# Batch 0's first tile alone and batch 1's expert tile by tile: another order for the first 48 slots of an attention and MLP kernel

## Chip, core and metric

The kernel runs on one core of a Trainium2 chip. The metric is the device time of one execution in microseconds (us). The engines are PE (TensorE, matmuls), DVE (VectorE), ACT (ScalarE), POOL (GpSimd, which here mostly issues loads) and SP (SyncE, which issues stores and DMA transposes). Each works through its own list of instructions in order and waits on semaphores for the others.

## What is computed

The inputs are q, k, v (8 batches, 8 heads, 576 rows, 64 columns), two vectors of gains and two weights, 512x2048 and 2048x512.

```python
kv = np.einsum('bhsd,bhse->bhde', k, v)
out = np.einsum('bhsd,bhde->bhse', q, kv)
rms = np.sqrt(np.mean(out * out, axis=-1, keepdims=True) + 1e-06)
x = out / rms * g_norm                     # heads side by side: (8, 576, 512)
...
xn = (x - mu) / np.sqrt(var + 1e-06) * g_ln
ch = np.maximum(xn @ w_ch1, 0.0) @ w_ch2
return x + ch
```

## The kernel before

**Tiles.** A batch's 576 rows make four tiles of 128 rows and a rest of 64; the rests of two batches share a tile of their own ("rem"). Per tile, `Tile` makes: `o` (four matmuls of q transposed with kv of a pair of heads), `sq` (square, ACT), `red` (sum per head, DVE), `root` (ACT), `inv` (reciprocal, DVE), `y` and `x` (scale by inverse root and by g_norm, DVE, with the sum for the mean), `xc` (minus mean, times g_ln, bf16, DVE), `var` (ACT), and `turn` (four transposes on PE into PSUM and an ACT copy to xT, or a DMA transpose). `o_g` with `x_g` is a shorter way for batch 0: kv is multiplied by g_norm beforehand (`kv_g`), so that one matmul and one DVE instruction give x.

**Expert.** `mm1` (line 402) multiplies xT by the first weight, in groups that fill one PSUM bank of 128x512 (16 matmuls of 128 columns for one tile, 8 of 256 columns for two tiles together), and ACT evicts each with Relu (line 405). `mm2_part` (line 418) multiplies by the second weight, 16 matmuls of 512 columns per tile, and `finish` (DVE, line 423) adds x and stores.

**Order.** It is written out by hand. `tick()` is called ahead of each group of the first product and each four matmuls of the second. Each call is a slot with a number; `at(slot, fn)` puts other work ahead of the slot's matmuls. A batch of four tiles takes 32 slots: 0 to 15 are the first product of batch 0, 16 to 31 its second product, 32 to 47 the first product of batch 1. `plan_tile(s, ...)` puts o, sq and red at slot s, y, x and xc at s + behind, var at s + 6, and turn at its own slot. `q_turns` transposes batch 1's q on PE, `kv_of` makes kv of a batch; both use the single PSUM bank of `ps_m` ("misc"), as `turn` does. `ps1` has three banks, `ps2` and `ps_out` two each.

**Start.** k comes by SP and ACT, cast on the chip; v and q by POOL in its queue (lines 126 to 132): v in two halves of two pairs of heads, q's lower part (five groups j of 64 rows, on partitions 0 to 63) in two halves of four heads, the first quarter of the first weight, q's upper part (four groups j, on partitions 64 to 127), the rest of the first weight, the second weight, batch 1. PE runs 18 matmuls whose result is not read (`fill`, line 196) until v is there. `kv_first` makes kv in two halves of two pairs. Tiles 0 and 1 of batch 0 then go side by side in halves of four heads: `half_turn` (q transposed), `half_o` (o and square), `half_red`; then root, o_g, x_g, and xc in halves of 256 columns (`halves_xc`, `halves_turn`). Tile i is made of two groups j: tile 0 of j 0 and 1, tile 1 of j 2 and 3 of the lower part; tiles 2 and 3 of the upper part. The fifth lower group is the rest J.

In slots 0 to 15 the first product of batch 0 runs over tiles 0 and 1 in pieces (`mm1(0, ts, 1, c0, c1)`), then tile 2, then tile 3. Slot 1 holds the turn of tile 2's q, tile 1's transposes, and tile 2's o to xc; slots 4 and 5 do the same for tile 3; slots 6 and 10 turn tiles 2 and 3; slot 9 turns J. Batch 1's tiles begin at slots 23, 25, 29 and 33 and are turned at 28, 31, 37 and 39; its first product takes tiles 0 and 1 together (slots 32 to 39), then 2 and 3 (slots 40 to 47).

Of the kernel before, what the change touches and what calls it, by code (L numbers as in the profile page):

```python
# [14 lines left out]
def kernel(  # L15
# [11 lines left out]
    nc = tc.nc  # L27
    f32 = mybir.dt.float32
    bf16 = mybir.dt.bfloat16
# [9 lines left out]
    nDe = Dh // 128  # L39
# [46 lines left out]
    def lo(t, b, h0=0, h1=H):  # L86
        return t[b, h0:h1, :S_LO, :].rearrange("h (p j) d -> p h j d", j=JJ)
# [29 lines left out]
    def pairs(t, hp0, hp1):  # L117
        return bass.AP(tensor=t.tensor, offset=t.offset + hp0 * 2 * S * D,
                       ap=[[JP * D, 128], [2 * S * D, hp1 - hp0], [1, JP * D]])
# [3 lines left out]
    nc.vector.memset(fill_sb, 0.0)  # L123
    nc.sync.dma_start(k_f[:, :HP // 2], pairs(k, 0, HP // 2))
    nc.scalar.dma_start(k_f[:, HP // 2:], pairs(k, HP // 2, HP))
    nc.gpsimd.dma_start(v_p[:, :HP // 2], pairs(v, 0, HP // 2))
    nc.gpsimd.dma_start(v_p[:, HP // 2:], pairs(v, HP // 2, HP))
    for h0 in (0, H // 2):
        nc.gpsimd.dma_start(q_in[0][:64, h0:h0 + H // 2], lo(q, 0, h0, h0 + H // 2))
    load_w1(0)  # L130
    make_identity(nc, identity)
    nc.gpsimd.dma_start(q_in[0][64:, :, :J], up(q, 0))
# [57 lines left out]
        n = turn_groups(tp, i, 0, H)  # L190
        copy(qts[0][:, i, :, :n], tp[:, :, :n])  # L191

    def fill(n, pool=ps2, tag="p2"):
        for _ in range(n):
            p1 = pool.tile([128, 512], f32, tag=tag, name="p1")
            nc.tensor.matmul(p1, lhsT=fill_sb[:, :128], rhs=fill_sb, start=True, stop=True)  # L196
            del p1

    def turn_q_dma(b):
        q_p = kv_in.tile([128, JJ, H, D], bf16, tag="qp", bufs=2)  # L200
# [3 lines left out]
            q_t.rearrange("p j hp t -> p (j hp) t"), q_p.rearrange("p j h d -> p (j h d)"))  # L204
        qts[b] = q_t

    def kv_first():
        kvp = held[0] = kv_pack[0]
        g = g_norm_sb.to_broadcast([128, HP // 2, D])
        for i, (pe, te, po, to) in enumerate(((ps_m, "misc", ps1, "p1"), (ps1, "p1", ps1, "p1"))):  # L210
            even = pe.tile([128, HP // 2, D], f32, tag=te, name="even")
            odd = po.tile([128, HP // 2, D], f32, tag=to, name="odd")
            hps = slice(i * HP // 2, (i + 1) * HP // 2)
            for hp in range(hps.start, hps.stop):
                for j in range(JP):
                    js = slice(j * D, (j + 1) * D)
                    for hh, dst in ((0, even), (1, odd)):
                        rows = slice(hh * D, hh * D + D)
                        nc.tensor.matmul(dst[rows, hp - hps.start, :], lhsT=k_p[rows, hp, js],
                                         rhs=v_p[rows, hp, js],  # L220
                                         start=(j == 0), stop=(j == JP - 1))
            nc.vector.tensor_copy(kvp[:D, hps, :D], even[:D])
            nc.scalar.copy(kvp[D:, hps, D:], odd[D:])
            nc.vector.tensor_mul(kv_g[:D, hps, :D], even[:D], g[:D])
            nc.vector.tensor_mul(kv_g[D:, hps, D:], odd[D:], g[D:])
            del even, odd

    def kv_of(b):
        kv_ps = ps_m.tile([128, HP, D], f32, tag="misc", name="kv_ps")
# [127 lines left out]
            blks["rem"] = new_block("rem", 1)  # L357
        return Tile(mms, blks["rem"], b // 2)

    def plan_tile(s, make, turn_at, on_pe, behind=2):  # L360
        box = []

        def first():
            t = make()
            box.append(t)
            t.o()
            t.sq()
            t.red()

        def second():  # L370
            t = box[0]
            t.y()
            t.x()
            t.xc()

        def third():
            box[0].var()

        def fourth():
            box[0].turn(on_pe)  # L380

        at(s, first)
        at(s + behind, second)
        at(s + 6, third)
        at(turn_at, fourth)

# [71 lines left out]
    def at(slot, fn):  # L458
        agenda.setdefault(int(slot), []).append((slot, fn))
# [12 lines left out]
    del gl_row  # L472

    qts[0] = qt_pool.tile([128, JJ, HP, 128], bf16, tag="qt", name="qt")
    fill(18)
    kv_first()


    t = [main_tile(0, i, ps2, "p2") for i in range(4)]
    for i in range(2):  # L480
        t[i].ss = work.tile([128, H, 1], f32, tag="ss", bufs=4, name="ss")
    sqs = [work.tile([128, H, D], f32, tag="sq", name="sq") for _ in range(2)]
    banks = (((ps_out, "ops"), (ps_m, "misc")), ((ps_out, "ops"), (ps1, "p1")))
    copies = ((nc.scalar.copy, nc.scalar.copy), (nc.vector.tensor_copy, nc.vector.tensor_copy))

    def half_turn(half):
        hp0 = half * HP // 2
        tps = [ps2.tile([128, HP // 2, 128], bf16, tag="p2", name="tp") for _ in range(2)]
        for i in range(2):
            turn_groups(tps[i], i, 2 * hp0, 2 * hp0 + H // 2)  # L490
        for i in range(2):
            copies[half][i](qts[0][:, i, hp0:hp0 + HP // 2], tps[i])

    def half_o(i, half):
        hp0 = half * HP // 2
        pool, tag = banks[half][i]
        o = pool.tile([128, H // 2, D], f32, tag=tag, name="o_half")
        flat = o.rearrange("p h e -> p (h e)")
        for k2 in range(HP // 2):
            nc.tensor.matmul(flat[:, k2 * 128:(k2 + 1) * 128], lhsT=qts[0][:, i, hp0 + k2, :],  # L500
                             rhs=kv_pack[0][:, hp0 + k2, :], start=True, stop=True)
        nc.scalar.activation(sqs[i][:, half * H // 2:(half + 1) * H // 2], o, func=AF.Square)

    def half_red(i, half):
        hs = slice(half * H // 2, (half + 1) * H // 2)
        nc.vector.tensor_reduce(t[i].ss[:, hs], sqs[i][:, hs], axis=AX.X, op=ALU.add)

    half_turn(0)
    fill(2, ps_out, "ops")
    half_o(0, 0)  # L510
    half_turn(1)
    half_o(1, 0)
    half_o(0, 1)
    half_red(0, 0)
    half_red(0, 1)
    half_o(1, 1)
    t[0].root()
    half_red(1, 0)
    half_red(1, 1)
    t[0].o_g(ps1, "p1")  # L520
    t[1].o_g(ps1, "p1")
    fill(8)
    t[0].x_g()
    t[1].root()


    def halves_xc(i):
# [5 lines left out]
                                           in1=g_ln_sb[:, cs], op0=ALU.add, op1=ALU.mult)  # L533
            yield xc

    def halves_turn(i, xcs, pool, tag):
        xT = t[i].blk[2]
        for c, xc in enumerate(xcs):
            tp = pool.tile([128, 2, 128], bf16, tag=tag, name="tp")
            for kk in range(2):  # L540
                nc.tensor.transpose(tp[:, kk, :], xc[:, kk * 128:(kk + 1) * 128], identity)
            nc.scalar.copy(xT[:, 2 * c:2 * c + 2, i * 128:(i + 1) * 128], tp)

    halves_turn(0, halves_xc(0), ps_out, "ops")
    t[1].x_g()
    xc1 = list(halves_xc(1))


    def x2():
        t[2].red()  # L550
        t[2].y()
        t[2].x()
        t[2].xc()

    def x3():
        t[3].sq()
        t[3].red()
        t[3].y()
        t[3].x()
        t[3].xc()  # L560

    def o2():
        t[2].o()
        t[2].sq()

    def next_loads():
        nc.gpsimd.memset(k_in[0][64:, :, J], 0.0)
        nc.gpsimd.memset(v_in[0][64:, :, J], 0.0)
        load_batch(2)

    at(1, lambda: turn_first(2, ps_m, "misc", nc.vector.tensor_copy))
    at(1.1, lambda: halves_turn(1, xc1, ps_out, "ops"))
    at(1.2, o2)
    at(1.3, x2)
    at(4, lambda: turn_first(3, ps_m, "misc"))
    at(5, lambda: t[3].o())
    at(5.1, x3)
    at(6, lambda: t[2].turn(True))
    at(9, lambda: turn_first(J, ps_m, "misc"))
    at(9.5, next_loads)  # L580
    at(10, lambda: t[3].turn(True))
    for i in range(4):
        at(16 + i, lambda i=i: t[i].var())
    at(20, lambda: (rstd_of(0), t.clear()))
# [2 lines left out]
    def q_turns(s, b):  # L587
        def start():
            q_ps[b] = kv_in.tile([128, JJ, H, D], bf16, tag="qp", bufs=2, name="q_p")
            nc.vector.tensor_copy(q_ps[b].rearrange("p j h d -> p h j d"), q_in[b % NB])  # L590
            qts[b] = qt_pool.tile([128, JJ, HP, 128], bf16, tag="qt", name="qt")
            turn_q(b, 0, ps_out, "ops")
            turn_q(b, 1, ps_out, "ops")

        at(s, start)
        for i, j in enumerate((2, 3, 4)):
            at(s + 1.5 + i, lambda j=j: turn_q(b, j, ps_m, "misc"))
        at(s + 4, lambda: q_ps.pop(b))

    at(21, lambda: kv_of(1))  # L600
    q_turns(21.5, 1)
    for j, s, behind, tn in ((0, 23, 1, 28), (1, 25, 1, 31), (2, 29, 2, 37), (3, 33, 2, 39)):
        plan_tile(s, lambda j=j: main_tile(1, j), tn, True, behind)
    at(46, lambda: rstd_of(1))

    at(36, lambda: kv_of(2))
# [19 lines left out]
    at(32 * B + 14, lambda: rstd_of("rem"))  # L626


    for ts, c0, c1 in ((0, 0, 8), (1, 0, 8), (0, 8, 12), (1, 8, 12), (0, 12, 16), (1, 12, 16),
                       (2, 0, 16), (3, 0, 16)):  # L630
        mm1(0, ts, 1, c0, c1)
    p2s = [ps1.tile([128, Dm], f32, tag="p1", name="p2") for _ in range(2)]
    p2s += [ps2.tile([128, Dm], f32, tag="p2", name="p2") for _ in range(2)]
    for ts in range(4):
        mm2_part(0, ts, p2s[ts], 0, nDe // 2)
    for ts in range(4):
        p2 = p2s[ts]
        p2s[ts] = None
        mm2_part(0, ts, p2, nDe // 2, nDe)
        finish(0, ts, p2)  # L640
        del p2
    del blks[0], m1s[0]
    mm1(1, 0, 2)
    mm1(1, 2, 2)
    mm2(1)
    mm1(2, 0, 2)
    mm1(2, 2, 2)
# [36 lines left out]
```

## Time and profile before

| | |
|---|---|
| median of three runs | 293.75 us (293.29, 293.94, 293.75) |
| the profiled execution | 293.29 us, of which the span of the profile is 291.2 us |
| DVE, ACT busy | 151.0 us, 155.8 us |
| PE, first product (line 402) | 889 matmuls recorded, 131.1 us |
| PE, second product (line 418) | 590 matmuls recorded, 126.6 us |
| granted TensorE clock | 1.00 in every stretch |
| first matmul of slot 0, 16, and o in slot 48 | 15.75, 33.34 and 68.20 us |

In a timeline each row is: start, duration, engine, line, operation, written tile <- read tiles, shapes, count; in brackets the idle time of the engine before it and what ended that. The duration of a row on PE includes the modelled tail of its last matmul, so that rows overlap. Some matmul records are missing, so counts can be one short. In the chain each row is: start, duration, and the engine, tile and line that the end depended on in that stretch.

### The profile page before, as it was taken

To read this page: it belongs to the slowest core of one execution; us is meant where nothing else is said; L and a number is where in the kernel's file an instruction comes from. 1 tells how busy PE (TensorE), PEld (TensorE's weight loads), DVE (VectorE), ACT (ScalarE), POOL (GpSimd) and SP (SyncE) were. 2 spreads that over 40 slices of the span, in tenths; PEclk is the share of its full clock that TensorE was granted. 3 is DMA by queue.
4 is the path that set the end of the run, shared out by engine and by line. 5 is a ranking of instruction groups with operands and counts; after the bars stand their busy time and mean duration, and the time that the engine had idled before them with its cause. 6 is when DMAs were issued, how large, how long until landed. Compare 5 with 4: busy or idle time off the path is not lost.

```text
span 291.2 us, 5506 instructions
## 1 busy us (share of the span) xinstructions
PE 280.6 (96%) x2158; PEld 156.8 (54%) x2184; DVE 151.0 (52%) x335; ACT 155.8 (54%) x339; POOL 41.3 (14%) x68
## 2 busy tenths in 40 slices
PE   8889999989999999999999999999999999999995
PEld 3579754876569744444444444444444444444444
DVE  5775029917997793576257935752578300220022
ACT  3467765776459841892189408930894066017500
POOL 8523520004014002300320014000000000000000
PEclk9999999999999999999999999999999999999999
DMA  7999999559999948994998279928202510131033
GB/s 214 203 206 203 201 202 203 114 92 150 168 192 137 166 60 147 200 172 85 138 211 118 56 139 174 201 60 168 66 18 44 120 36 0 38 75 33 0 73 74
DMA packets 64377, 36.08 MB, mean 124 GB/s; under 512 B 31836, under 2 KB 59356, under 8 KB 64352
## 3 DMA queue, kind: packets, MB, share of 16 engines
q0 software_dynamic: 28016, 17.76, 43.4%
q1 hardware_dynamic: 35824, 17.25, 30.5%
q10 hardware_dynamic: 512, 0.72, 0.8%
q8 instruction: 17, 0.28, 0.4%
q14 instruction: 8, 0.07, 0.1%
HBM read 36.71 MB, written 9.44 MB: 158 GB/s over the span
## 4 chain that ended last, share of the span: by engine, by line
PE 87%; DVE 5%; DMA 2%; ACT 2%; issue 1%; POOL 1%; DVEq 0%; POOLq 0%
PE p L402 40%; PE p L418 40%; PE o_ps L260 3%; DMA q_in<-in_q_dram 2%; PE kv_ps L235 2%; DVE o_sb L423 1%; DVE ss L287 1%; DVE xc L321 1%; DVE x_blk L311 1%; DVE y L292 1%; PE tp L183 1%; ACT m L405 1%; PE p L196 1%; PE tp L337 0%; PE tp L170 0%
## 5 line engine op out<-in xcount | busy, mean ns | idle before, releaser
L402 PE MATMUL p<-xT_blk,w_sb 128*128 128x512 bf16 (+2 forms) x889 | 131.1, 302 | 1.4 <-ACT xT_blk L339 0.8
L418 PE MATMUL p<-w_sb,m 128*128 128x512 bf16 (+2 forms) x590 | 126.6, 368 | 1.5 <-issue 0.8
L405 ACT ACTIVATE m<-p 128x512 bf16<-128x512 f32 x144 | 85.5, 596 | 44.2 <-PE p L402 42.1
L402 PEld LDWEIGHTS <-w_sb 128*128 128x128 bf16 x896 | 76.1, 98 | 46.3 <-issue 1.6
L418 PEld LDWEIGHTS <-m 128*128 128x128 bf16 x608 | 57.0, 98 | 61.8
L423 DVE SCALAR_TENSOR_TENSOR o_sb<-p,rstd,x_blk 128x512 f32<-128x512 f32 (+2 forms) x38 | 27.4, 721 | 53.2 <-PE p L418 50.3
L266 ACT ACTIVATE sq<-o_ps 128x512 f32<-128x512 f32 x34 | 20.2, 594 | 40.6 <-PE o_ps L260 40.5
L287 DVE TENSOR_REDUCE ss<-sq 128x8 f32<-128x512 f32 x34 | 23.1, 678 | 14.0 <-ACT sq L266 14.0
L329 ACT ACTIVATE dev<-x_blk,st_blk 128x512 f32<-128x512 f32 x36 | 25.7, 715 | 5.1 <-DVE st_blk L315 4.9
L321 DVE SCALAR_TENSOR_TENSOR xc<-x_blk,st_blk,g_ln_sb 128x512 bf16<-128x512 f32 x34 | 25.6, 752 | 1.2
L292 DVE TENSOR_TENSOR y<-o_ps,inv 128x512 f32<-128x512 f32 x34 | 23.5, 692 | 3.1
L311 DVE SCALAR_TENSOR_TENSOR x_blk<-y,g_norm_sb 128x512 f32<-128x512 f32 x34 | 23.5, 692 | 1.2
L411 DVE RECIPROCAL rstd<-rstd 128x4 f32<-128x4 f32 x9 | 1.6, 174 | 35.2 <-ACT rstd L410 35.2
L304 DVE RECIPROCAL inv<-rms 128x8 f32<-128x8 f32 x36 | 7.2, 201 | 22.9 <-ACT rms L297 22.9
L98 POOL COPY gate<-qt 1x1 bf16<-1x1 bf16 x5 | 0.9, 178 | 115.6 <-DMA qt<-q_p 115.6
L297 ACT ACTIVATE rms<-ss,eps_sb 128x8 f32<-128x8 f32 x36 | 10.7, 297 | 10.3 <-DVE ss L287 9.6
L260 PEld LDWEIGHTS <-qt 128*128 128x128 bf16 (+1 forms) x152 | 9.8, 100 | 7.1 <-issue 1.7
L260 PE MATMUL o_ps<-kv_pack,qt 128*128 128x128 bf16 (+1 forms) x152 | 13.3, 220 | 0.3 <-DVE qt L191 0.2
L196 PE MATMUL p<-fill_sb 128*128 128x512 bf16 x27 | 8.5, 476 | 1.4 <-DVE eps_sb L137 1.2
L329 ACT ACTIVATION_READ_ACCUMULATOR dev<-x_blk,st_blk 128x1 f32 x36 | 6.8, 190 | 0.0
L235 PEld LDWEIGHTS <-k_in 128*64 128x64 bf16 x280 | 5.0, 112 | 2.8 <-issue 2.8
L238 ACT CAST kv_pack<-kv_ps 64x256 bf16<-64x256 f32 x7 | 2.6, 365 | 7.2 <-PE kv_ps L235 7.2
(79 smaller groups left out, 117.4 us busy)
## 6 DMA issues: line engine op xcount, KB each, us to landing
out_dram<-o_sb SPq DMA_DIRECT2D x70, 128.0 KB, 2.4
w_sb<-in_moe_w_ch_dram POOLq DMA_DIRECT2D x8, 512.0 KB, 14.3
k_in<-in_k_dram POOLq DMA_DIRECT2D x7, 320.0 KB, 5.9
v_in<-in_v_dram POOLq DMA_DIRECT2D x7, 320.0 KB, 9.6
q_in<-in_q_dram POOLq DMA_DIRECT2D x7, 320.0 KB, 12.7
q_in<-in_q_dram POOLq DMA_DIRECT2D x8, 256.0 KB, 13.2
k_in<-in_k_dram POOLq DMA_DIRECT2D x7, 256.0 KB, 7.0
v_in<-in_v_dram POOLq DMA_DIRECT2D x7, 256.0 KB, 10.9
```

Source lines behind the costliest of these rows:

```text
L196: nc.tensor.matmul(p1, lhsT=fill_sb[:, :128], rhs=fill_sb, start=True, stop=True)
L260: nc.tensor.matmul(flat[rows, hp * 128:(hp + 1) * 128], lhsT=lhsT_of(hp), rhs=kvp[:, hp, :], start=True, stop=True)
L266: nc.scalar.activation(self.sq_t, self.o_ps, func=AF.Square)
L287: nc.vector.tensor_reduce(self.ss, self.sq_t, axis=AX.X, op=ALU.add)
L292: nc.vector.tensor_mul(self.y_t, self.o_ps, self.inv().to_broadcast([128, H, D]))
L311: nc.vector.scalar_tensor_tensor(x_blk[:, ts].rearrange("p (h d) -> p h d", h=H), in0=self.y_t, scalar=1.0, in1=g_norm_sb.to_broadcast([12 ...
L321: nc.vector.scalar_tensor_tensor(self.xc_t, in0=x_blk[:, self.ts], scalar=st[:, 1, self.ts:self.ts + 1], in1=g_ln_sb, op0=ALU.add, op1=ALU ...
L329: nc.scalar.activation(dev, x_blk[:, ts], func=AF.Square, bias=st[:, 1, ts:ts + 1], accum_out=st[:, 2, ts:ts + 1])
L402: nc.tensor.matmul(p1[:, i, :], lhsT=w1_sb[:, kk, de * 128:(de + 1) * 128], rhs=blk[2][:, kk, sl], start=(kk == 0), stop=(kk == nK - 1))
L405: nc.scalar.activation(m1[:, de0:de0 + per, sl], p1, func=AF.Relu)
L418: nc.tensor.matmul(p2[:, c0:c1], lhsT=m1s[b][:, de, ts * 128:(ts + 1) * 128], rhs=w2_sb[:, de, c0:c1], start=(de == 0), stop=(de == nDe - 1))
L423: nc.vector.scalar_tensor_tensor(o_sb[:, c0:c1], in0=p2[:, c0:c1], scalar=rstds[b][:, ts:ts + 1], in1=blks[b][0][:, ts, c0:c1], op0=ALU.mu ...
```

## The change

1. Loads: v comes as three pairs of heads and one pair; between the two, q's groups j 0 and 1 of all heads; after the last pair, q's groups j 2 to 4.
2. `kv_first` becomes the class `KvFirst`: three pairs (kv_a), then tile 0's turn of q, one fill, and the last pair (kv_b).
3. Tile 0 goes alone, its o, square and reduce in parts of three pairs and one pair. Tile 1's q is turned behind tile 0's o; its o, square and o_g, and the turn of J, stand behind tile 0's o_g with three and five fills around; its reduce comes behind tile 0's xc.
4. Slot 1 turns q of tiles 2 and 3 at once, tile 1's two halves (the second copied by DVE) with tile 2's o between them, and ends with tile 2's root. Tile 2 goes by o_g and x_g (slot 2). Tile 3's o to xc come right behind tile 2's turn (slot 5), its turn at slot 11. Slots 4, 6, 9 and 10 become empty.
5. Batch 0's first product takes tiles 0 and 1 in quarters, tile 2 from slot 6, tile 3 from slot 12. Its second product goes in a half and two quarters in place of two halves.
6. Batch 1: the turns of q at 23 instead of 21.5 with the second in "misc"; tiles begin at 24, 27, 31 and 35, the second part always two slots behind, turns at 30, 34, 38 and 42; the first product tile by tile (128 columns a matmul).

```diff
-    nc.gpsimd.dma_start(v_p[:, :HP // 2], pairs(v, 0, HP // 2))
-    nc.gpsimd.dma_start(v_p[:, HP // 2:], pairs(v, HP // 2, HP))
-    for h0 in (0, H // 2):
-        nc.gpsimd.dma_start(q_in[0][:64, h0:h0 + H // 2], lo(q, 0, h0, h0 + H // 2))
+    nc.gpsimd.dma_start(v_p[:, :HP - 1], pairs(v, 0, HP - 1))
+    nc.gpsimd.dma_start(q_in[0][:64, :, :2], lo(q, 0)[:, :, :2])
+    nc.gpsimd.dma_start(v_p[:, HP - 1:], pairs(v, HP - 1, HP))
+    nc.gpsimd.dma_start(q_in[0][:64, :, 2:], lo(q, 0)[:, :, 2:])
...
+    kv_a = KvFirst(0, HP - 1, ((ps_m, "misc"), (ps1, "p1")))
+    kv_b = KvFirst(HP - 1, HP, ((ps1, "p1"), (ps1, "p1")))
+    t = [main_tile(0, 0)] + [main_tile(0, i, *((ps1, "p1") if i == 1 else (ps2, "p2")))
+                             for i in range(1, 4)]
...
+    kv_a.mms()
+    kv_a.copies()
+    turn_first(0, ps2, "p2")
+    kv_a.times_g()
+    fill(1)
+    kv_b.mms()
+    kv_b.copies()
+    part_o(kv_a)
+    part_o(kv_b)
+    part_sq(kv_a)
+    part_sq(kv_b)
+    kv_b.times_g()
+    part_red(kv_a)
+    part_red(kv_b)
+    turn_first(1, ps_m, "misc")
     t[0].root()
-    half_red(1, 0)
-    half_red(1, 1)
-    t[0].o_g(ps1, "p1")
+    t[0].o_g(ps2, "p2")
+    dead = fill(3)
+    t[1].o()
+    t[1].sq()
+    turn_first(J, ps_m, "misc")
     t[1].o_g(ps1, "p1")
-    fill(8)
+    fill(5, dead)
+    del dead
     t[0].x_g()
-    t[1].root()
...
+    for c, xc in enumerate(halves_xc(0)):
+        half_turn(0, c, xc, nc.scalar.copy)
+    t[1].red()
     t[1].x_g()
     xc1 = list(halves_xc(1))
...
+    def before_1():
+        turn_first(2, ps_m, "misc")
+        tp = ps2.tile([128, HP, 128], bf16, tag="p2", name="tp")
+        turn_groups(tp, 3, 0, H)
+        half_turn(1, 0, xc1[0], nc.scalar.copy)
+        t[2].o()
+        half_turn(1, 1, xc1[1], nc.vector.tensor_copy)
+        t[2].sq()
+        nc.scalar.copy(qts[0][:, 3], tp)
+        t[2].red()
+        t[2].root()
+        del tp, xc1[:]
+
+    def before_2():
+        t[2].o_g(ps2, "p2")
+        t[2].x_g()
+        t[2].xc()
...
-    at(1, lambda: turn_first(2, ps_m, "misc", nc.vector.tensor_copy))
-    at(1.1, lambda: halves_turn(1, xc1, ps_out, "ops"))
-    at(1.2, o2)
-    at(1.3, x2)
-    at(4, lambda: turn_first(3, ps_m, "misc"))
-    at(5, lambda: t[3].o())
-    at(5.1, x3)
-    at(6, lambda: t[2].turn(True))
-    at(9, lambda: turn_first(J, ps_m, "misc"))
+    at(1, before_1)
+    at(2, before_2)
+    at(5, lambda: t[2].turn(True))
+    at(5.1, before_5)
     at(9.5, next_loads)
-    at(10, lambda: t[3].turn(True))
+    at(11, lambda: t[3].turn(True))
...
-            turn_q(b, 1, ps_out, "ops")
+            turn_q(b, 1, ps_m, "misc")
...
-    q_turns(21.5, 1)
-    for j, s, behind, tn in ((0, 23, 1, 28), (1, 25, 1, 31), (2, 29, 2, 37), (3, 33, 2, 39)):
-        plan_tile(s, lambda j=j: main_tile(1, j), tn, True, behind)
+    q_turns(23, 1)
+    for j, s, tn in ((0, 24, 30), (1, 27, 34), (2, 31, 38), (3, 35, 42)):
+        plan_tile(s, lambda j=j: main_tile(1, j), tn, True)
...
-    for ts, c0, c1 in ((0, 0, 8), (1, 0, 8), (0, 8, 12), (1, 8, 12), (0, 12, 16), (1, 12, 16),
-                       (2, 0, 16), (3, 0, 16)):
+    for ts, c0, c1 in ((0, 0, 4), (1, 0, 4), (0, 4, 8), (1, 4, 8), (0, 8, 12), (1, 8, 12),
+                       (2, 0, 12), (0, 12, 16), (1, 12, 16), (2, 12, 16), (3, 0, 16)):
         mm1(0, ts, 1, c0, c1)
...
-    for ts in range(4):
-        mm2_part(0, ts, p2s[ts], 0, nDe // 2)
+    for de0, de1 in ((0, nDe // 2), (nDe // 2, nDe * 3 // 4)):
+        for ts in range(4):
+            mm2_part(0, ts, p2s[ts], de0, de1)
     for ts in range(4):
         p2 = p2s[ts]
         p2s[ts] = None
-        mm2_part(0, ts, p2, nDe // 2, nDe)
+        mm2_part(0, ts, p2, nDe * 3 // 4, nDe)
         finish(0, ts, p2)
         del p2
     del blks[0], m1s[0]
-    mm1(1, 0, 2)
-    mm1(1, 2, 2)
+    for ts in range(4):
+        mm1(1, ts, 1)
     mm2(1)
```

`part_o`, `part_sq` and `part_red` do for the pairs of one `KvFirst` what `half_o` and `half_red` did for a half. `before_5` is tile 3's o, sq, red, y, x and xc. `fill` returns its PSUM tile, so that a later call can go on in the same one.

## The prediction, made before the result was known

> **What bounds it.** I read the page first, then the timeline of the start, TensorE's timeline from 33 to 69 us, and the chain in that stretch. A slot is the work of one tick(): 16 matmuls of one tile's first product, or four of the second.
>
> ```profile
> PE 280.6 (96%) x2158; PEld 156.8 (54%) x2184; DVE 151.0 (52%) x335; ACT 155.8 (54%) x339; POOL 41.3 (14%) x68
> ...
> PE 87%; DVE 5%; DMA 2%; ACT 2%; issue 1%; POOL 1%; DVEq 0%; POOLq 0%
> ```
>
> TensorE (PE) is the bound, but its busy share counts each matmul's modelled tail, so its stalls are read between rows. The chain shows where others decide: the loads and the norm chain of the start, and a stretch near 43 to 61. From 68.2 us on nothing of the change touches the order, and PE's rows follow on each other: whatever is won or lost by slot 48 passes to the end one for one.
>
> The start, from the timeline of all engines:
>
> ```profile
> 9.78 0.44 PE L183 MATMUL tp<-identity,q_in 64*64 64x64 bf16 x16
> ...
> 13.54 0.69 DVE L278 SCALAR_TENSOR_TENSOR x_blk<-og_ps,inv 128x512 f32<-128x512 f32 x1
> ...
> 15.01 0.68 PE L541 MATMUL tp<-identity,xc 128*128 128x128 bf16 x4 [0.84 <-DVE xc L532]
> ...
> 15.75 1.34 PE L402 MATMUL p<-xT_blk,w_sb 128*128 128x128 bf16 x16
> ...
> 18.23 2.84 PE L402 MATMUL p<-xT_blk,w_sb 128*128 128x128 bf16 x48
> ```
>
> To be seen: q's first half lands at 9.7, tile 0's x_g starts at 13.54, slot 0 at 15.75, slot 1 at 18.23. PE's timeline of the next stretch:
>
> ```profile
> 33.34 4.48 PE L418 MATMUL p<-w_sb,m 128*128 128x512 bf16 x19
> ...
> 47.53 1.89 PE L418 MATMUL p<-w_sb,m 128*128 128x512 bf16 x8
> 49.84 0.40 PE L337 MATMUL tp<-identity,xc 128*128 128x128 bf16 x4 [0.42 <-DVE xc L321]
> ...
> 55.51 1.05 PE L402 MATMUL p<-xT_blk,w_sb 128*128 128x256 bf16 x8
> 57.00 0.38 PE L337 MATMUL tp<-identity,xc 128*128 128x128 bf16 x4 [0.45 <-ACT kv_pack L239]
> ...
> 59.19 1.04 PE L402 MATMUL p<-xT_blk,w_sb 128*128 128x256 bf16 x8
> 60.99 3.65 PE L402 MATMUL p<-xT_blk,w_sb 128*128 128x256 bf16 x32 [0.76 <-ACT xT_blk L339]
> ...
> 64.71 3.66 PE L402 MATMUL p<-xT_blk,w_sb 128*128 128x256 bf16 x32
> 68.20 0.39 PE L260 MATMUL o_ps<-kv_pack,qt 128*128 128x128 bf16 x4
> ```
>
> Three stalls, larger than their labels since the label ends where the tail does. Start to start, 128x512 takes 0.216 us and 128x256 takes 0.109 (32 between 64.71 and 68.20). So 47.53 + 8 x 0.216 = 49.26, and the turn comes at 49.84: 0.58. 55.51 + 0.87 = 56.38 to 57.00: 0.62. 59.19 + 0.87 = 60.06 to 60.99: 0.93. Together **2.13 us**. The chain of that stretch says why:
>
> ```profile
> 42.42 0.59 ACT qt L173
> ...
> 43.59 0.70 DVE y L292
> ...
> 45.24 0.75 DVE xc L321
> 45.99 0.60 DVE ss L287
> 46.59 0.66 DVE o_sb L423
> ...
> 54.25 0.66 DVE o_sb L423
> 54.91 0.60 DVE ss L287
> ```
>
> VectorE (DVE) works without a gap from 43.28 to 58.58 on batch 1's four tiles and batch 0's four finishes; PE catches up with it at slots 31, 37 and 40.
>
> **Start: loads.** The same bytes in another order. v's halves (288 KB each) release PE at 7.49 and 8.93: 0.72 per pair of heads. q's first 160 KB take 0.85 more (9.78); the second half is turned at 10.80, so at most 1.02. After: v's three pairs 7.49 + 0.72 = 8.21. Then q's j 0 and 1, 128 KB: by bytes 0.68 to 0.82; by pieces (512, a q half has 256) 1.7 to 2.0. I take 1.0, near the bytes, as v's pieces of nearly twice a q piece's size take nearly twice as long: 9.2. v's last pair 9.9. q's rest, 192 KB in 512 pieces: 1.0 to 1.2 or 1.7 to 2.0; I take 1.2: 11.1 (ends 10.6 and 12.6 or so). POOL has one issue in each place as before (0.65 to 0.83 each); w1's chunks and q's upper part slip by 2.2 - 1.87 = 0.33. Slot 1 now needs chunk 0 only; tile 2's turn needs the upper part, whose landing releases POOL at 15.81 now: 16.15, wanted at 16.3.
>
> [...] The new pieces are 256 and 384 B in SBUF; no row of before has such q pieces. [...]
>
> **Start: chain.** Turn of tile 0 at 9.2 (0.44), ACT copy 0.58: to 10.3. The last pair's 18 matmuls 9.95 to 10.4 (16 ns apart, 0.19 tail), ACT's copy (about 0.21, from 0.26 for 128 columns and 0.37 for 256) to 10.65. Squares of 384 and 128 columns, between and below 0.39 for 256 and 0.59 for 512: about 0.46 and 0.29, to 11.4. Reduces (0.41 for 256, 0.69 for 512) about 0.55 and 0.27: to 12.0. Meanwhile tile 1's turn waits for q's rest, 11.1 to 11.55, and its ACT copy, 11.6 to 12.17, stands ahead of the root on ACT: root to 12.47, inverse, x_g at **12.8** instead of 13.54. Slot 0 then ends 0.74 earlier, at 16.3.
>
> Tile 1 pays: its o, square and reduce are no longer beside tile 0's. Reduce after tile 0's second xc half (14.6) to 15.2; root behind tile 0's xT copies (15.37) to 15.67; x_g at 16.0 (was 15.57), xc halves done at 17.45 and 17.8. PE meanwhile does both turns of tiles 2 and 3 (2 x 0.37, to 17.0), waits 0.45, and ends slot 1 at 19.3; before it was 18.23 + 0.89 = 19.1. So +0.15. From there to slot 16 PE drops tile 3's turn (0.37) and J's (0.24, now in the wait for tile 0's root) and gains o_g of tile 2 (0.22) with some 0.1 of wait for tile 3's copy: -0.3. Rows also show 0.45 of stalls there (23.62 + 48 x 0.056 = 26.30, next row 26.61; small ones besides); more time to each chain should end two thirds: -0.3. Fill matmuls are 27 for 28, all in waits: nothing. **Start: -0.45** (by bytes -0.75, by pieces +1.05).
>
> **Batch 1 tile by tile.** 256 matmuls of 128 columns at 5.36 / 96 = 0.0558 (27.98 to 33.34), for 128 at 0.109: 14.28 - 13.95 = **+0.33**. Evictions stay 16 of 128x512. In return tiles 1, 2, 3 are first read at slots 36, 40, 44 (were 32, 40, 40) and turned at 34, 38, 42 (were 31, 37, 39); kv_of(2) at 36 has two slots before the next use of its bank, was one. Is everything in time? Slot 16 at 32.9; slot 24 brings tile 0's o one slot later, and its root stands behind two q copies on ACT, one of which waited for the single "misc" bank (PE +0.16 there): DVE's chain starts at 43.9, later than 43.28, and does the same work at the same rows: xc of tile 1 done 50.5, tile 2's reduce 52.4, xc of tile 2 55.7, of tile 3 59.9 (batch 2's q copy, 0.82, goes ahead of it now). PE reaches slot 32 at 49.8, the turns at 51.6, 56.35 and 60.1: margins 1.1, 0.6, 0.2. Slots 33 and 34 take the PSUM banks of finishes 0 and 1, free at 47.9 and 51.2, wanted at 50.7 and 51.8. ACT, back to back from 52.4 (eviction 0.49 start to start as 53.98 to 54.48; xT copy, square the same, casts 0.75, dev 0.70, root 0.22), ends tile 2's copy at 58.3, needed 58.4. So nearly all 2.13 goes, and what is late next is ACT's xT copy and tile 3's xc, by margins under 0.3; I leave 0.2 for them. **Stage: -2.13 + 0.33 + 0.16 + 0.2 = -1.44** (-1.8 if nothing is late; +0.5 if every stall returns elsewhere). Second-product quarters in place of halves only move finishes to slots 28 to 32; w2's last chunk is needed later than now.
>
> **Sum.** -0.45 - 1.44 = -1.9 on the profiled execution's 293.29 (span 291.2 and 2.1 around it): 291.4. That run is the lowest of three and 0.46 below the median 293.75; I add half of it: **291.6**.
>
> **Rivals.** A, q's pieces cost by number: start +1.05, stage kept: -0.4, 293.1 by the same step. For: pieces double; against: v and q rows go nearly by bytes. B, the stalls move: DVE's chain begins later and ACT is full, so the 2.13 returns at slots 40 and 44: -0.45 + 0.5, 293.3. For: margins of 0.1 and 0.2; against: PE may wait there only by what is missing, not by 2. C, nothing is late: -0.75 - 1.8, 290.9. D, slower: TensorE's clock falls in the thin stretch of 16.3 to 18.5, where PE has turns, one o and a wait. Price: the first fills run 0.427 apart until 5.45, then 0.216, so half speed; a spell as long as that first one (4.2 us) costs 2.1 and only cancels the gain; it decides from 3.8 us on, and two such spells in dense slots give 295.8. Against: after the sparse 7.49 to 12.2 and 14.2 to 15.7 of now, matmuls still run at 0.216 and 0.056, and the granted clock reads 1.00 throughout.
>
> [...]
>
> **Numbers.** Forecast 0.60, A 0.13, B 0.12, C 0.09, D 0.06. 0.2% (about 0.6 us) is what a measurement of this kernel can tell from no change. Faster: forecast, C, and half of A and B, 0.81; same: the rest of A and B, 0.12; slower: D and a little, 0.07. Range 290.4 to 293.4: C to B; D and ends beyond are left out.
>
> **To look for.** v's matmuls at 8.2, tile 0's turn near 9.2, x_g near 12.8, slot 1's end near 19.3, the first second-product matmul near 32.9, no wait over 0.3 between 49 and 62, second product of batch 1 near 66.5 (68.20 + 0.22 now). Wrong would be: turns of tile 1 after 12 (A), waits at slots 40 or 44 (B), matmuls 0.11 apart after 18 (D).

## The result, and the profile after

The changed kernel takes **290.89 us** (median of four runs, 290.85 to 290.94); the kernel before took 293.53 in the four runs beside them (293.29 to 293.94). The ratio is 0.9909, with a 95% interval of 0.9891 to 0.9926. The profiled execution took 290.94 us with a span of 289.2. Forecast were 291.6 us, and 290.4 to 293.4 as the range.

First the page's line of busy time and its shares of the chain:

```profile
PE 279.8 (97%) x2289; PEld 158.9 (55%) x2315; DVE 149.8 (52%) x331; ACT 155.4 (54%) x338; POOL 40.9 (14%) x68
...
PE 91%; DMA 2%; DVE 2%; ACT 2%; issue 1%; DVEq 0%; POOLq 0%
```

PE is busy for 0.8 us less in a span 2 us shorter, though it has more instructions. DVE's share of the chain falls from 5% to 2% with its busy time almost as it was: what went is DVE's work on the path. The timeline of the start, all engines:

```profile
9.12 0.41 PE L183 MATMUL tp<-identity,q_in 64*64 64x64 bf16 x14
...
10.79 0.44 PE L183 MATMUL tp<-identity,q_in 64*64 64x64 bf16 x16
...
12.66 0.69 DVE L288 SCALAR_TENSOR_TENSOR x_blk<-og_ps,inv 128x512 f32<-128x512 f32 x1
...
14.88 1.34 PE L412 MATMUL p<-xT_blk,w_sb 128*128 128x128 bf16 x16
...
17.23 0.29 PE L553 MATMUL tp<-identity,xc 128*128 128x128 bf16 x2 [0.39 <-DVE xc L546]
...
17.98 1.26 PE L412 MATMUL p<-xT_blk,w_sb 128*128 128x128 bf16 x16
...
19.07 0.39 PE L282 MATMUL og_ps<-kv_g,qt 128*128 128x128 bf16 x4
```

Tile 0's turn of q is at 9.06 (its first matmul is a row of its own), tile 1's at 10.79 with no wait in brackets, x_g at 12.66, slot 0 at 14.88 (15.75 before). Slot 1 comes at 17.98 and ends at 19.07. Then PE's timeline from slot 16 to slot 48:

```profile
32.91 4.48 PE L428 MATMUL p<-w_sb,m 128*128 128x512 bf16 x19
...
49.93 1.95 PE L412 MATMUL p<-xT_blk,w_sb 128*128 128x128 bf16 x32
51.72 0.39 PE L347 MATMUL tp<-identity,xc 128*128 128x128 bf16 x4
...
56.60 0.39 PE L347 MATMUL tp<-identity,xc 128*128 128x128 bf16 x4
56.82 3.74 PE L412 MATMUL p<-xT_blk,w_sb 128*128 128x128 bf16 x64
60.39 0.39 PE L347 MATMUL tp<-identity,xc 128*128 128x128 bf16 x4
60.62 1.95 PE L412 MATMUL p<-xT_blk,w_sb 128*128 128x128 bf16 x32
...
66.20 0.39 PE L270 MATMUL o_ps<-kv_pack,qt 128*128 128x128 bf16 x4
```

The three turns have no bracket: 49.93 + 32 x 0.0558 = 51.72, just where the turn of tile 1 stands. The chain of waits in that stretch, where DVE's steps stood from 43.59 and from 54.25 on before, is PE alone from 42.67 on, but for 0.05 of issue:

```profile
41.55 0.60 ACT sq L276
42.15 0.48 ACT qt L173
42.63 0.04 issue
42.67 0.38 PE tp L170 x4
...
50.09 1.79 PE p L412 x32
51.88 0.22 PE tp L347 x4
...
54.87 1.89 PE p L412 x32
56.76 0.22 PE tp L347 x4
56.98 3.57 PE p L412 x64
60.56 0.22 PE tp L347 x4
```

Where the 2.35 us between the two profiled executions come from:

| | before | after | gained |
|---|---|---|---|
| up to slot 16 | 33.34 | 32.91 | 0.43 |
| slot 16 to the o of slot 48 | 34.86 | 33.29 | 1.57 |
| from there to the end of the span | 223.0 | 223.0 | 0 |
| time around the span | 2.09 | 1.74 | 0.35 |

### The profile page after: what moved, and what is told of

Read it like the earlier page. It is cut to its first block, busy times and chain, and to the rows that moved or that the text cites. A ratio compares the mean times of both kernels' runs of the same rounds, so it can differ in the third digit from the quotient of the medians.

```text
span 289.2 us, 5765 instructions
## 1 busy us (share of the span) xinstructions
PE 279.8 (97%) x2289; PEld 158.9 (55%) x2315; DVE 149.8 (52%) x331; ACT 155.4 (54%) x338; POOL 40.9 (14%) x68
## 4 chain that ended last, share of the span: by engine, by line
PE 91%; DMA 2%; DVE 2%; ACT 2%; issue 1%; DVEq 0%; POOLq 0%
PE p L428 43%; PE p L412 42%; PE o_ps L270 3%; DMA v_in<-in_v_dram 2%; PE kv_ps L245 2%; ACT m L415 1%; DVE x_blk L288 0%; DVE xc L546 0%; PE tp L347 0%; ACT sq L276 0%; ACT xT_blk L349 0%; PE tp L170 0%; ACT rms L307 0%; DVE ss L512 0%; PE tp L553 0%
## 5 line engine op out<-in xcount | busy, mean ns | idle before, releaser
L412 PE MATMUL p<-xT_blk,w_sb 128*128 128x128 bf16 (+2 forms) x1017 | 131.4, 285 | 0.8
L415 ACT ACTIVATE m<-p 128x512 bf16<-128x512 f32 x144 | 85.4, 596 | 43.9 <-PE p L412 41.8
L412 PEld LDWEIGHTS <-w_sb 128*128 128x128 bf16 x1024 | 78.6, 98 | 44.5 <-issue 1.1
L276 ACT ACTIVATE sq<-o_ps 128x512 f32<-128x512 f32 x35 | 20.9, 596 | 42.1 <-PE o_ps L270 42.1
L297 DVE TENSOR_REDUCE ss<-sq 128x8 f32<-128x512 f32 x35 | 23.7, 678 | 11.4 <-ACT sq L276 11.4
L302 DVE TENSOR_TENSOR y<-o_ps,inv 128x512 f32<-128x512 f32 x33 | 22.8, 692 | 3.0
L321 DVE SCALAR_TENSOR_TENSOR x_blk<-y,g_norm_sb 128x512 f32<-128x512 f32 x33 | 22.8, 692 | 1.1
L197 PE MATMUL p<-fill_sb 128*128 128x512 bf16 x26 | 7.8, 449 | 1.3 <-DVE eps_sb L137 1.2
```

Source lines behind the costliest of these rows:

```text
L276: nc.scalar.activation(self.sq_t, self.o_ps, func=AF.Square)
L297: nc.vector.tensor_reduce(self.ss, self.sq_t, axis=AX.X, op=ALU.add)
L302: nc.vector.tensor_mul(self.y_t, self.o_ps, self.inv().to_broadcast([128, H, D]))
L321: nc.vector.scalar_tensor_tensor(x_blk[:, ts].rearrange("p (h d) -> p h d", h=H), in0=self.y_t, scalar=1.0, in1=g_norm_sb.to_broadcast([12 ...
L412: nc.tensor.matmul(p1[:, i, :], lhsT=w1_sb[:, kk, de * 128:(de + 1) * 128], rhs=blk[2][:, kk, sl], start=(kk == 0), stop=(kk == nK - 1))
L415: nc.scalar.activation(m1[:, de0:de0 + per, sl], p1, func=AF.Relu)
```

## The experiments

Theory: two gains that add up, the start's by an earlier x_g and the stage's because batch 1's tiles are asked for later. Rivals: that one part alone carries the gain, or that an edit priced at nothing does work. Ratios are against runs of the kernel before on the same chip.

**1. The start alone.** The changed kernel with the old schedule of the second product and of batch 1:

```diff
-    q_turns(23, 1)
-    for j, s, tn in ((0, 24, 30), (1, 27, 34), (2, 31, 38), (3, 35, 42)):
+    q_turns(21.5, 1)
+    for j, s, behind, tn in ((0, 23, 1, 28), (1, 25, 1, 31), (2, 29, 2, 37), (3, 33, 2, 39)):
...
+    mm1(1, 0, 2)
+    mm1(1, 2, 2)
```

> The changed start and the changed slots 0 to 15, with batch 1's dates, its first product in pairs of tiles and batch 0's second product in halves as before. Theory, two gains that add and pass to the end one for one: slot 16 at 32.9 as in the changed kernel (33.34 before), the three stalls of 0.58, 0.62 and 0.93 still there between 49 and 61, span 290.7 (0.43 under 291.2). Rival, the start's gain is waited away again in slots 21 to 48, since VectorE's chain sets that stretch: slot 48 at 68.2 and span 291.2.

Measured: 292.85 us (12 runs), ratio 0.9982 (0.9968 to 0.9996). Of the 0.54 us between the medians some 0.35 lie around the span (experiment 9). Slot 16 is at 32.97, 0.37 earlier, but the o of slot 48 at 68.05, only 0.15 earlier. Its timeline, all engines, shows who took the rest:

```profile
37.47 0.83 DVE L608 COPY q_p<-q_in 128x2560 bf16<-128x2560 bf16 x1 [0.35 <-DMA q_in<-in_q_dram]
...
38.36 0.62 PE L170 MATMUL tp<-identity,q_p 128*128 128x128 bf16 x8 [0.16 <-DVE q_p L608]
...
49.70 0.40 PE L347 MATMUL tp<-identity,xc 128*128 128x128 bf16 x4 [0.42 <-DVE xc L331]
...
56.85 0.38 PE L347 MATMUL tp<-identity,xc 128*128 128x128 bf16 x4 [0.44 <-ACT kv_pack L249]
...
60.84 3.65 PE L412 MATMUL p<-xT_blk,w_sb 128*128 128x256 bf16 x32 [0.76 <-ACT xT_blk L349]
```

Batch 1's q lands at 37.13 in the changed kernel and at 36.99 in the kernel before: the load doesn't come earlier because PE does. Here its cast on DVE starts at 37.47, with the load in its bracket (37.41 before, with none). With the turn of q in slot 21.5, PE is there at 38.13 (37.38 + 0.75 for kv's 40 matmuls) and waits until 38.36; before, it came at 38.50 and didn't wait. So 0.23 of the 0.37 stay at this place. The landing isn't the only limit of the cast: from the start of the instruction ahead (the reciprocal of batch 0's rstd) to the cast, DVE takes 0.47 in the changed kernel, where the cast starts 0.23 behind the landing, 0.49 in experiments 3 and 6, where the profile shows nothing that it waits for, and 0.10 in the kernel before. By that gap alone, whose cause no run shows, the cast would have started at about 37.42 here (an estimate from 36.94 + 0.48). Theory half failed: the start's gain passes on in full only when batch 1's dates move too.

**2. Batch 1 alone.** The kernel before with the new dates, the tile-by-tile product, the "misc" bank and the quarters:

```diff
-    q_turns(21.5, 1)
+    q_turns(23, 1)
...
-    mm1(1, 0, 2)
-    mm1(1, 2, 2)
+    for ts in range(4):
+        mm1(1, ts, 1)
```

> The kernel before with only batch 1's new dates, its first product tile by tile, its second q turn in the bank misc, and batch 0's second product in a half and two quarters. Theory, two gains that add: slot 16 at 33.3, none of the three stalls, slot 48 some 1.6 earlier than before, at 66.6, span 289.6. Rival, the stage's gain needs the earlier start: VectorE's chain then ends too late for the turns at slots 38 and 42, at least 0.5 of the stalls comes back, span 290.1 or more.

Measured: 291.72 us (6 runs), ratio 0.9937 (0.9917 to 0.9958). PE's timeline has the three turns of batch 1 without a wait, and slot 48's o 1.53 earlier than before:

```profile
52.19 0.39 PE L337 MATMUL tp<-identity,xc 128*128 128x128 bf16 x4
...
57.06 0.39 PE L337 MATMUL tp<-identity,xc 128*128 128x128 bf16 x4
...
60.86 0.39 PE L337 MATMUL tp<-identity,xc 128*128 128x128 bf16 x4
...
66.67 0.39 PE L260 MATMUL o_ps<-kv_pack,qt 128*128 128x128 bf16 x4
```

The stage carries its gain alone. On top of it the start is worth 66.67 - 66.20 = 0.47 in full.

**3. Old dates, finer product.** The changed kernel with the dates, the "behind" and the PSUM bank of before, but still tile by tile.

```diff
-    q_turns(23, 1)
-    for j, s, tn in ((0, 24, 30), (1, 27, 34), (2, 31, 38), (3, 35, 42)):
+    q_turns(21.5, 1)
+    for j, s, behind, tn in ((0, 23, 1, 28), (1, 25, 1, 31), (2, 29, 2, 37), (3, 33, 2, 39)):
```

> The changed kernel, batch 1's first product still tile by tile, but with the old dates: q turns from 21.5, tiles at 23, 25, 29, 33, turns at 28, 31, 37, 39. Theory, the later dates take away the first two stalls and the finer product only the third: PE waits for tile 1's xc at slot 31 (0.6 to 0.9) and for the bank of kv_of(2) at slot 37 (about 0.6), but not at slot 40; span 290.4 to 290.9. Rival, the finer product alone gives the slack: no wait over 0.3, span 289.2 to 289.5.

Measured: 293.3 us (12 runs, 293.14 to 293.75), ratio 0.9989 (0.9978 to 1.0). PE's timeline, from the profiled run of 293.75, in which v landed 0.56 late and slot 16 stands at 33.49:

```profile
47.87 1.89 PE L428 MATMUL p<-w_sb,m 128*128 128x512 bf16 x8
50.06 0.40 PE L347 MATMUL tp<-identity,xc 128*128 128x128 bf16 x4 [0.30 <-DVE xc L331]
...
55.80 1.07 PE L412 MATMUL p<-xT_blk,w_sb 128*128 128x128 bf16 x16
57.88 0.38 PE L347 MATMUL tp<-identity,xc 128*128 128x128 bf16 x4 [1.01 <-ACT kv_pack L249]
...
60.11 4.63 PE L412 MATMUL p<-xT_blk,w_sb 128*128 128x128 bf16 x80
65.21 0.40 PE L270 MATMUL o_ps<-kv_pack,qt 128*128 128x128 bf16 x4 [0.47 <-DMA qt<-q_p]
```

Start to start, PE loses 0.46 ahead of tile 1's turn (47.87 + 8 x 0.216 = 49.60), 1.19 ahead of tile 2's (55.80 + 16 x 0.0558 = 56.69) and 0.64 ahead of the o of slot 44 (60.11 + 80 x 0.0558 = 64.57): 2.29 together, for 2.13 before. The wait at slot 40 is gone, as expected, but a third one stands at slot 44 in its place: batch 2's q, cast on DVE at 58.49 with these dates in the kernel before (56.05 in the changed kernel), comes out of its DMA transpose too late (0.47 in the row's bracket). The expectation missed that, and the size of the second wait (0.6): the spans are 291.4 to 291.9, not 290.4 to 290.9. So the finer product alone gains nothing. Dates, "behind" and bank went back together here, so their shares aren't separated. The later dates without the finer product can't be run: with two tiles at a time, slot 32 reads tile 1, whose turn would only stand at slot 34.

**4. The second product in halves again.**

```diff
-    for de0, de1 in ((0, nDe // 2), (nDe // 2, nDe * 3 // 4)):
-        for ts in range(4):
-            mm2_part(0, ts, p2s[ts], de0, de1)
+    for ts in range(4):
+        mm2_part(0, ts, p2s[ts], 0, nDe // 2)
...
-        mm2_part(0, ts, p2, nDe * 3 // 4, nDe)
+        mm2_part(0, ts, p2, nDe // 2, nDe)
```

> The changed kernel with batch 0's second product in two halves again, so that the four finishes fall at slots 26, 28, 30 and 32. Theory, only the finishes move, on VectorE, and TensorE is not held by them: span 289.2 within 0.2. Rival, the quarters are needed for the second weight's last chunk, which lands near 42: with halves slot 25 waits for it, span 289.5 or more.

Measured: 291.36 us (290.9 to 292.0, 6 runs), ratio 0.9922 (0.9901 to 0.9943). Its profile has slot 48's o at 66.23, as with quarters (66.20). The spread is wider (1.1 us against 0.1), with medians 0.5 apart; where the longer runs lose their time isn't settled.

**5. j 3's turn of q in another bank.** In the changed kernel the turn at 42.67 stands 0.23 behind PE (41.58 + 4 x 0.216 = 42.44), since its single "misc" bank is still read by ACT's copy (42.15 in the chain above).

```diff
-            at(s + 1.5 + i, lambda j=j: turn_q(b, j, ps_m, "misc"))
+            at(s + 1.5 + i, lambda j=j: turn_q(b, j, *((ps_out, "ops") if j == 3 else (ps_m, "misc"))))
```

> The changed kernel with the turn of batch 1's q group 3 (slot 25) in a bank of ps_out in place of misc. Theory, the waits of 0.23 at 42.67 and 0.10 at 43.85 are for the one bank misc, and go: span 289.0 to 288.9. Rival, the copies on ScalarE stand in order anyway and the wait moves to the next user of the bank: span 289.2.

Measured: **290.70 us** (290.61 to 290.72, 5 runs), ratio 0.9897 (0.9879 to 0.9915); the changed kernel on the same chip:

> The changed kernel once more, for the spread of its runs beside the runs of the kernel before. Theory, with its unread matmuls the clock does not fall: all runs within 0.3 of 290.9 and a mean granted clock of 0.998 or more, while some of the kernel before show 0.994 and about 1.3 more time. Rival, both kernels show such runs alike.

Measured: 290.84 us (290.83 to 290.95, 5 runs), ratio 0.9904 (0.9886 to 0.9921). PE's timeline of the version with the other bank:

```profile
41.60 1.03 PE L428 MATMUL p<-w_sb,m 128*128 128x512 bf16 x4
42.46 0.39 PE L170 MATMUL tp<-identity,q_p 128*128 128x128 bf16 x4
...
66.00 0.39 PE L270 MATMUL o_ps<-kv_pack,qt 128*128 128x128 bf16 x4
```

The gap is gone. From slot 16 (32.93) to the o of slot 48 it is 33.07 us, for 33.28 in the changed kernel beside it (32.84 to 66.12): 0.21 less. This version beats both kernels, the changed one by a small 0.14 us; no run of the one reaches into the runs of the other.

**6. The old load order.**

```diff
-    nc.gpsimd.dma_start(v_p[:, :HP - 1], pairs(v, 0, HP - 1))
-    nc.gpsimd.dma_start(q_in[0][:64, :, :2], lo(q, 0)[:, :, :2])
-    nc.gpsimd.dma_start(v_p[:, HP - 1:], pairs(v, HP - 1, HP))
-    nc.gpsimd.dma_start(q_in[0][:64, :, 2:], lo(q, 0)[:, :, 2:])
+    nc.gpsimd.dma_start(v_p[:, :HP // 2], pairs(v, 0, HP // 2))
+    nc.gpsimd.dma_start(v_p[:, HP // 2:], pairs(v, HP // 2, HP))
+    for h0 in (0, H // 2):
+        nc.gpsimd.dma_start(q_in[0][:64, h0:h0 + H // 2], lo(q, 0, h0, h0 + H // 2))
```

> The changed kernel with the loads of v and q in the old order: v in two halves, q's lower part in two halves of four heads. Theory, the order of the loads is what lets tile 0 go alone: its turn waits for q's second half, near 10.7 in place of 9.06, and its x_g starts near 14.3 in place of 12.66; the loss passes to the end, span 290.7 (1.5 over 289.2). Rival, it is the order of the chain that counts and the loads are hidden: x_g within 0.3 of 12.66, span under 289.6.

Measured: 293.18 us (292.11 to 294.88, 12 runs), ratio 0.9985 (0.9962 to 1.0008). PE's timeline:

```profile
10.61 0.32 PE L183 MATMUL tp<-identity,q_in 64*64 64x64 bf16 x8 [0.55 <-DMA q_in<-in_q_dram]
...
16.15 1.34 PE L412 MATMUL p<-xT_blk,w_sb 128*128 128x128 bf16 x16
```

Tile 0 alone needs all heads of two groups j, so by halves of four heads it waits for all of q's lower part: slot 0 is 1.27 late, and the end with it. The profiled run is one of three near 292.1, with a mean granted clock of 0.999 or 1.0; six runs lie at 293.05 to 293.37 with 0.993 or 0.994, three at 294.59 to 294.88 with 0.988. The latter nine are runs in which the clock fell for a while, though all the unread matmuls are there; the next two experiments are about that.

**7. Without the nine later unread matmuls.** The 18 first ones stay.

```diff
-    fill(1)
...
-    dead = fill(3)
...
-    fill(5, dead)
-    del dead
```

> The changed kernel without the nine unread matmuls after the first eighteen. Theory, they only pass the time and TensorE's clock holds without them: spans of single rows as in the changed kernel, matmuls of 128 columns 0.056 apart in slot 0 and later, span 289.2 within 0.2. Rival, they hold the clock: without them the sparse stretch from 9.5 to 15 lets it fall, matmuls of 128 columns stand 0.107 apart for up to 4.2 us, span 290.2 to 291.3.

Measured: 293.24 us (291.77 to 293.97, 12 runs), ratio 0.9981 (0.9961 to 1.0001). The view by stretches of 2 us (columns: stretch and its length, busy time with instruction counts of PE, PE's weight loads, DVE, ACT and POOL, granted clock, DMA share, GB/s) of this kernel:

```profile
12.00:14.00 2.00, 1.31 (x22) 0.82 (x20) 1.50 (x4) 1.81 (x5) 0.49 (x1) 1.00 1.37 202
14.00:16.00 2.00, 0.98 (x6) 0.56 (x7) 1.77 (x6) 0.63 (x2) 0.68 (x1) 0.83 1.26 204
16.00:18.00 2.00, 1.87 (x25) 1.64 (x25) 1.48 (x6) 0.46 (x3) 0.68 (x1) 0.50 1.24 205
18.00:20.00 2.00, 2.00 (x42) 1.69 (x37) 0.53 (x3) 1.67 (x4) 0.68 (x1) 0.50 1.24 206
20.00:22.00 2.00, 1.83 (x19) 1.72 (x17) 1.11 (x3) 1.13 (x4) 0.68 (x1) 0.50 1.24 206
22.00:24.00 2.00, 2.00 (x37) 2.00 (x35) 1.57 (x4) 1.16 (x2) 0.55 (x1) 0.96 1.27 215
```

and of the changed kernel:

```profile
12.00:14.00 2.00, 2.00 (x22) 1.05 (x21) 1.47 (x6) 1.16 (x3) 0.52 (x1) 1.00 1.36 200
14.00:16.00 2.00, 1.66 (x21) 1.16 (x20) 1.50 (x5) 0.94 (x3) 0.21 (x2) 1.00 1.28 208
16.00:18.00 2.00, 1.54 (x45) 1.15 (x43) 1.55 (x6) 1.52 (x4) 0.63 (x1) 1.00 1.24 206
```

PE's timeline shows it in the matmuls:

```profile
15.66 2.16 PE L412 MATMUL p<-xT_blk,w_sb 128*128 128x128 bf16 x16
...
35.77 0.38 PE L428 MATMUL p<-w_sb,m 128*128 128x512 bf16 x1
```

Without the unread matmuls the clock stands at 0.50 for 6.84 us (0.68 in 14 to 16, 6.0 in 16 to 22, 0.16 in 22 to 24), and slot 0 to slot 16 takes 20.11 us for 18.03: **2.08 lost**. (Slot 0 itself is 0.78 later here because v landed at 9.05 for 8.27 in this run.) Over the twelve runs, a mean clock of 0.992 to 0.994 goes with 291.8 us, 0.988 with 292.7 to 294.0, 0.982 with 293.6 to 294.0.

**8. Which of the nine.** Without the last five, and without the first four:

```diff
-    fill(5, dead)
```

> The changed kernel without the last five of its nine later unread matmuls (those behind tile 1's o_g, while PE waits for tile 0's x_g and xc). Without all nine, the profiled execution's granted clock fell to 0.50 for 16 to 22 us and the runs spread over 291.8 to 294.0. Theory (these five carry the clock, since they stand in the longest gap, about 12.7 to 14.2): the clock falls here too in part of the runs, median 292 to 293.5, slot 16 in a profile that shows it 1 to 2 us later than 32.9, mean clock of the run 0.994 or lower. Rival (PE must only not be empty for long anywhere, the one and the three ahead are enough): clock 1.00 throughout, median 290.8 to 291.2, spread as of the changed kernel (290.83 to 290.95).

```diff
-    fill(1)
...
-    dead = fill(3)
...
-    fill(5, dead)
-    del dead
+    fill(5)
```

> The changed kernel without the first four of its nine later unread matmuls (the one ahead of v's last pair and the three behind tile 0's o_g); the five before tile 0's transposes stay, in a PSUM tile of their own. Theory (the five carry the clock): clock 1.00, median 290.8 to 291.2. Rival (all nine together keep PE busy enough): the clock falls in part of the runs, median 291.5 to 293.5, mean clock of those runs 0.994 or lower.

Measured: without the five, 290.98 us (6 runs, ratio 0.9929, 0.9902 to 0.9956): four runs at 290.85 to 291.02 with a clock of 0.998 or more, one at 291.92 with 0.994, one at 293.32 with 0.988. Without the four, 291.12 us (290.88 to 291.52, 5 runs, ratio 0.9915, 0.99 to 0.9929), all at 1.00. The five guard the clock, as the theory said, but its median was wrong: without them the clock falls now and then, not mostly. Two falls in six runs are few, but in the 49 runs with the new load order and the five (changed kernel, experiments 1, 3, 4, 5 and the one without the four) no mean clock was under 0.998. The four first ones were needed in none of five runs. With the old load order all nine were not enough: the clock fell in nine of the twelve runs of experiment 6.

**9. The time around the span.** The kernel before, the unread matmuls of one call in one PSUM tile:

```diff
+        p1 = pool.tile([128, 512], f32, tag=tag, name="p1")
         for _ in range(n):
-            p1 = pool.tile([128, 512], f32, tag=tag, name="p1")
             nc.tensor.matmul(p1, lhsT=fill_sb[:, :128], rhs=fill_sb, start=True, stop=True)
-            del p1
+        del p1
```

> The kernel before, with the unread matmuls of one call all in one PSUM tile instead of a new tile each (18, 2 and 8 of them); nothing else. It asks where the 0.4 us around the profile's span went (2.13 to 2.18 in every run with the old start, 1.73 to 1.80 in every run with the new one). Theory (it isn't the unread matmuls' tiles): time about 293.4, 2.15 around the span. Rival (it is these tiles and their releases): 1.75 around the span, time about 293.0.

Measured: 293.58 us (8 runs), ratio 1.0001 (0.9991 to 1.0012), 2.11 to 2.18 around the span: not these tiles.

## Why the prediction was right, and where it wasn't

**Loads.** Right in order, and better than taken: v's first matmul 8.27 (8.2 forecast), tile 0's turn 9.06 (9.2), tile 1's turn 10.79 with no wait for a DMA (11.1). So q's 128 KB in 256 B pieces took 0.79 us behind v, the by-bytes end of 0.68 to 0.82. Rival A (by pieces) fell. The pieces are 256 B in SBUF but 512 B at the source, where q is f32, so no run here says anything of shorter reads.

**Start, -0.45; measured -0.43,** but two of its terms were off and cancelled. Slot 1 ended at 19.07 for the forecast 19.3: from the old 19.12 that is -0.05, where I had +0.15. The stretch from there to slot 16 gained 0.38 (13.84 for 14.22), where I had -0.3 for the moved turns and -0.3 for "two thirds" of 0.45 of small stalls. The moved turns gave all of the 0.38; **the stalls stayed**, 0.44 in sum in both kernels. In the changed one they are 22.43 + 96 x 0.0558 = 27.79, next row 28.02, and 28.24 + 80 x 0.0558 = 32.70, next row 32.91. The waits of PE's weight loads between 18 and 34 us (us in total, times, longest) show no chain behind them:

```profile
PEld L412 <- issue: 0.7, 4, 0.2
```

"Issue" means that the engine waited for nothing that the profile shows. I had put these gaps down to chains that more time would relieve; what makes them stays open.

**Stage, -1.44; measured -1.57.** The three stalls of 2.13 went, all of them. The +0.33 for narrower matmuls fits the rows (62.63 to 66.20 is 3.57 for four slots, 64.71 to 68.20 was 3.49), and the +0.16 for j 3's bank was near (0.21 by experiment 5). The 0.2 for ACT's xT copy and tile 3's xc was not needed: -2.13 + 0.33 + 0.21 = -1.59. Rival B (the stalls move) fell, by the margins forecast: DVE's chain began at 43.91 (43.9), tile 1's xc ended at 50.42 (50.5), tile 2's reduce at 52.33 (52.4) and xc at 55.53 (55.7), ACT's copy for slot 40 at 58.35 (58.3). Tile 3's xc ended at 60.13 (59.9) for a turn at 60.39 (60.1): both later by about 0.25, so the margin of 0.2 held. Experiment 2 shows that this part gains by itself, experiment 3 that it needs the dates. That the two parts add up hid a condition that the sum doesn't have: the start's 0.43 reaches the end in full only because the same edit moves batch 1's q turns from slot 21.5 to 23, away from the cast of q at 37.4 (experiment 1).

**The sum's last step failed.** In the span the two terms give -1.9, and -2.0 was measured. The other 0.6 us of the miss are around it: I took the 2.1 us around the span for constant, and they became 1.74; and I added 0.2 to come nearer to the median, which the changed kernel's runs, all within 0.1 us, didn't ask for. Every kernel with the new start has 1.73 to 1.85 around its span, with old loads and without unread matmuls too (experiments 6, 7); the kernel before, experiment 2 and experiment 9 have 2.1 to 2.2. So the new start does it, but neither its loads nor its unread matmuls; what does stays open.

**"Fill matmuls are 27 for 28, all in waits: nothing."** Wrong as a judgement, harmless in the sum. As time they cost nothing; what they do is hold the clock. Rival D was therefore nearer than its 0.06 says: its mechanism is real, and in this load order the unread matmuls are what keeps it away. It named the wrong stretch: in experiment 7 the clock fell near 15.3, behind the thin stretch of 12 to 15.3 that the unread matmuls had filled, and in the changed kernel the stretch from 16 to 18 ran at 1.00. Its price was too high: a spell of 6.84 us cost 2.08, or 0.30 per us, not the half that full slots would pay; a likely reason, not tested, is that the same stretch of the changed kernel has waits for DVE (0.39 at 17.23) which a slower PE fills. At that rate, an estimate, the spell that cancels the gain of 1.9 is some 6.3 us, not 3.8. My evidence against it, the sparse stretches of before, was weak: 5 of the 29 runs of before beside experiments 1, 2, 6 and 7 had a mean clock of 0.994 and took 294.57 to 295.1, and the others 293.18 to 293.98. In the nine runs of the changed kernel the clock was never under 0.998.

**Slips in the working.** Rival B's 293.3 lacks the 0.2 that the other times have; with it B stands at 293.5, outside the range that it was to bound. DVE was not without a gap from 43.28 to 58.58: up to 55.87 it waits 0.37 for ACT's root. And PE caught up with DVE itself only at slot 31; the brackets of the second and third stall name ACT, which stands behind DVE's reduce in the second (0.25 at 55.53) and works without a gap from 59.17 on in the third. The new dates ended all three, so the sum didn't depend on it. "The granted clock reads 1.00 throughout", and the table of the kernel before, don't hold for the first 5.4 us: the clock column reads 1.00 there too, while the rows stand 0.427 apart.

Rival C (nothing late) named the measured time, 290.9, but by another way: a start of -0.75, which wasn't there.

## What to carry to other kernels

A stall in which a full engine catches up with a busy one was cured here by dates: ask for the late thing in smaller pieces, so that the last piece is needed later, then move its producers; the smaller pieces alone gave nothing (experiment 3). A start that gets faster passes its gain on only as far as the next thing that doesn't come earlier with it, here the cast of the next batch's q behind its load, so look for the first wait behind it. Before an unread matmul is counted as free or removed, read the granted clock of the stretch that it stands in, over several runs.

## What the runs showed of the hardware

The granted clock fell after a thin stretch in which PE was not idle: in experiment 7 PE has 1.31 us of busy time, tails included, in 12 to 14 and 0.98 in 14 to 16, and the clock drops near 15.3. (The first of experiment 8 had 1.05 in 12 to 14 and 1.56 in 14 to 16 in its profiled run, and the clock held.) The mean clocks come in steps, near 0.994, 0.988 and 0.982; a spell of T us at half speed in 292 us gives 1 - 0.5 T / 292, so the steps would be spells of about 3.5, 7 and 10.5 us (an estimate from these means), and the one that the profile shows is 6.84, with a mean of 0.988. (A mean of 0.998 or 0.999 went with no loss of time: in the first of experiment 8 a run at 0.998, the profiled one, and a run at 1.00 both took 290.94 us, and the profile reads 1.00 in every stretch from 8 to 24; in experiment 6 the runs at 0.999 took 292.17 and the one at 1.00 took 292.11.) Why the clock fell in two of the six runs of the first of experiment 8 and held in the other four, and how thin a stretch must be for a fall, no run here shows.

Batch 1's q lands at 36.99 in the kernel before, whose slot 16 stands at 33.34, and at 37.13 in the changed kernel with slot 16 at 32.91; in experiment 1, with slot 16 at 32.97, its cast starts at 37.47. This queue of loads kept its own time, whatever PE gained.

The same first load lands at different times: in seven profiled runs with the new load order v's first matmul is at 8.19 to 8.37, in two others at 8.83 and 9.05, and slot 0 moves with it (14.80 to 14.98, 15.45 and 15.66). In the eight of them whose clock held, slot 16 stands 24.64 to 24.66 behind that matmul. A part of each kernel's spread may be that; the runs without a profile don't show it.
